# Top-k attention and a PReLU MLP in one kernel: when pairs are prepared and how the MLP's steps are paced

## The chip, the core and the metric

The kernel runs on one core of a Trainium2 chip. The metric is the device time of one execution in microseconds (us). The engines are PE (TensorE, matrix products), DVE (VectorE), ACT (ScalarE), POOL (GpSimd) and SP (SyncE, which here only issues DMAs). Each works off its own queue in order; they wait for each other through semaphores.

## The reference

```python
def _attn_ref(q, k, v):                     # 8 batches, 8 heads, 576 rows, head size 64
    scores = scale * np.matmul(q, k.transpose(0, 1, 3, 2))
    kth = np.partition(scores, -top_k, axis=-1)[..., -top_k:-top_k + 1]      # top_k = 32
    mask = scores >= kth
    scores = np.where(mask, scores, -1000000000.0)
    scores = scores - np.max(scores, axis=-1, keepdims=True)
    attn = np.exp(scores)
    attn = attn / (np.sum(attn, axis=-1, keepdims=True) + 1e-09)
    return np.matmul(attn, v)
def _moe_ref(x, w_in, w_out, alpha):        # x: 4608 tokens of 512; 2048 hidden
    h = x @ w_in
    g = np.maximum(h, 0.0) + alpha * np.minimum(h, 0.0)
    return g @ w_out
```

The attention's output, with its heads side by side, is the x of the MLP.

## The kernel before, in words

**Pairs, rows and ticks.** Two heads make a pair; there are 32 pairs, four to a batch. A pair has nine row blocks of 128 rows (four for each head, and a ninth made of the last 64 rows of both), so there are 288 row blocks. The program is written out by hand as a loop over ticks n (line 753). In tick n each engine gets its part for the row block that has reached it: PE the scores of block n+1 (line 314, two blocks at once, but the ninth of a pair alone), ACT the biased copy b (323), the sign count h (329) and the exponential e (334) of block n, POOL the sign SG, DVE the flip y of block n-1 (345), the segment maxima of block n-2 (355), the merge to the top values of block n-3 (370, 372), and the mask of block n-7 (419), which POOL multiplies with e (429). SP then transposes the weights by DMA, and three or four ticks later PE forms their product with v, av, into pu (488); DVE takes the reciprocal rz of the sums (505) and ACT writes the scaled result to xb (517). Within a tick PE's queue holds first the scores, then the step of the MLP, then everything that is listed for that tick under "pe": the preparation and the av products. On DVE the work listed under "dve" stands near the end of the tick, just ahead of the flip.

**Preparation.** `prep_plan(p)` lists 17 steps for a pair, each at a number of ticks before BASE[p], the due tick: transposes of q and k into qkT on PE with copies by ACT (lines 175 to 201, -14 to -11), a product of k with itself pg (206, -11) and its copy GK, the product pr of GK with q (218, -10), DVE's product P (226, -9), the statistics st (234, -7), and eight tiny DVE steps up to -2, which give NT, the estimate of each row's threshold that b needs. The loads of q and k are issued 18 ticks before BASE, those of v 13. BASE is 9p up to pair 27. Row blocks 252 to 287 belong to the last batch, whose four pairs are worked through side by side in an order of their own (ORDER, line 152); their due ticks are 247, 250, 254 and 258. qkT has 5 buffers, v 6, the staging tiles 2.

**The MLP.** `back` is a queue of steps. Each step has a PE part and an ACT part, `after`, which is run at the head of the next tick or just ahead of the next step. First come the steps that load and scale the weights; the last four, `w_id`, each add up 16 products into pl (596), and `w_id2` copies pl to w_id_b (600). Then come blocks of 512 or 128 tokens: `ph` steps (635), each four products of 512 columns, followed by ACT's gT (641), and after them, for each 128 tokens, three `pz` steps of up to seven products (649, 653), the last of them followed by ACT's copy o_sb (658) and the store. A 512-token block has 16 ph and 12 pz steps, a 128-token block 4 and 3. ph and pz share one PSUM bank, so that a step waits for the copy of the one before. Up to tick 251 every tick takes one step; from tick 252 a credit of 1.9 a tick (2.4 from tick 288) is spent at 0.9 for a ph and 1.5 for a pz.

**From attention to MLP.** When the last pair of a batch is finished, `x_turn` has SP transpose its xb by five DMAs into xT, the operand of ph (line 721, tick n+7), and `feed` appends the blocks that are complete to `back` (722, tick n+8), so that their first step stands one tick after that.

Of the kernel before, what the change touches and what calls it, by code (L numbers as in the profile page):

```python
# [16 lines left out]
S = 576  # L17
# [13 lines left out]
def kernel(  # L31
# [17 lines left out]
    NPAIR = (B * H) // 2  # L49
# [107 lines left out]
    while n < NT:  # L157
# [2 lines left out]
            unit_of[n + i] = (n, m, i)  # L160
        units.append((n, m))
        n += m
    BASE = {p: TPP * p for p in range(P0)}
    BASE.update({P0: N0 - 5, P0 + 1: N0 - 2, P0 + 2: N0 + 2, P0 + 3: N0 + 6})

    def prep_plan(p):
        d = pairs[p]
# [387 lines left out]
    def weight_steps():  # L555
        hold = {}

        def alpha():
            a16 = mlp.tile([NFT, 128], FP32, name="a16", bufs=1)
            nc.sync.dma_start(a16, moe_alpha.rearrange("(t p) -> t p", p=128))  # L560
            hold["a16"] = a16

        def alpha1():
            aps = ps_m.tile([128, NFT], FP32, name="aps", tag="misc")
            nc.tensor.transpose(aps, hold["a16"], ident_f[0:NFT, 0:NFT])
            hold["aps"] = aps
            hold["inT"] = mlp.tile([128, NKT, NFT, 128], BF16, name="w_inT", tag="gT", bufs=1)

        def alpha2():
            nc.scalar.copy(alpha_sb, hold["aps"])  # L570
            nc.gpsimd.tensor_scalar(alpha1m, alpha_sb, -1.0, 1.0, ALU.mult, ALU.add)

        def lin(f):
            return xT[:, f // 4, DM * (f % 4):DM * (f % 4 + 1)]

        def w_in(kk):
            for hf in range(0, DFF, 1024):
                nc.gpsimd.dma_start(w_in_b[:, kk, hf:hf + 1024],
                                    moe_w_in[kk * 128:(kk + 1) * 128, hf:hf + 1024])

        def w_in2(kk):
            nc.sync.dma_start_transpose(hold["inT"][:, kk, :, :], w_in_b[:, kk, :])

        def w_out(f):
            hold[f] = mlp.tile([128, DM], FP32, name="w_stage2", tag="stage", bufs=3)
            nc.sync.dma_start(hold[f], moe_w_out[f * 128:(f + 1) * 128, :])

        def w_out2(f):
            ws = hold.pop(f)
            nc.scalar.activation(w_out_b[:, f, :], ws, AF.Copy, scale=alpha1m[:, f:f + 1])  # L590
            nc.scalar.activation(lin(f), ws, AF.Copy, scale=alpha_sb[:, f:f + 1])

        def w_id(kk):
            hold["pl"] = pl = ps_m.tile([128, DM], FP32, name="pl", tag="misc")
            for f in range(NFT):
                nc.tensor.matmul(pl, hold["inT"][:, kk, f, :], lin(f),
                                 start=(f == 0), stop=(f == NFT - 1))

        def w_id2(kk):
            nc.scalar.copy(w_id_b[:, kk, :], hold["pl"])  # L600

        yield alpha, None
        yield (lambda: None), None
        yield (lambda: (alpha1(), w_out(0), w_out(1))), alpha2
        for f in range(NFT):
            yield ((lambda f=f: (w_out(f + 2) if f + 2 < NFT else None,
                                 w_in(f // 2) if f < 8 and f % 2 == 0 else None)),
                   (lambda f=f: w_out2(f)))
            yield (lambda: None), (lambda f=f: w_in2(f // 2) if f < 8 and f % 2 == 1 else None)
        for kk in range(NKT):  # L610
            yield (lambda kk=kk: w_id(kk)), (lambda kk=kk: w_id2(kk))

    banks = [0, 0]

# [8 lines left out]
    def mlp_steps(t0, tb):  # L623
        c0 = t0 % NX
        fpp = 512 // tb if tb <= 256 else 1
        hold = {}

        def ph_step(f):
            if f == 0:
                hold["gT"] = mlp.tile([128, NFT, 512], BF16, name="gT", tag="gT", bufs=1)  # L630
            ph = mlp_bank("ph", fpp * tb)
            hold[f] = ph.rearrange("p (f t) -> p f t", f=fpp)
            for i in range(fpp):
                for kk in range(NKT):
                    nc.tensor.matmul(hold[f][:, i, :],  # L635
                                     w_in_b[:, kk, (f + i) * 128:(f + i + 1) * 128],
                                     xT[:, kk, c0:c0 + tb],
                                     start=(kk == 0), stop=(kk == NKT - 1))

        def ph_act(f):  # L640
            nc.scalar.activation(hold["gT"][:, f:f + fpp, 0:tb], hold.pop(f), AF.Relu)  # L641

        def pz_step(r0, m, part):
            if part == 0:
                hold["pz"] = mlp_bank("pz", DM)
            pz = hold["pz"]
            for i in range(part * 7, min(part * 7 + 7, NKT + NFT)):
                if i < NKT:
                    nc.tensor.matmul(pz[0:m], xT[:, i, c0 + r0:c0 + r0 + m],  # L649
                                     w_id_b[:, i, :], start=(i == 0), stop=False)  # L650
                else:
                    f = i - NKT
                    nc.tensor.matmul(pz[0:m], hold["gT"][:, f, r0:r0 + m], w_out_b[:, f, :],  # L653
                                     start=False, stop=(f == NFT - 1))

        def pz_act(r0, m):
            o_sb = mlp.tile([128, DM], FP32, name="o_sb", tag="stage", bufs=3)
            nc.scalar.copy(o_sb[0:m], hold["pz"][0:m])  # L658
            if t0 == t7 - 64:
                nc.sync.dma_start(out[t0:t7, :], o_sb[0:64])  # L660
                nc.sync.dma_start(out[NTOK - 64:NTOK, :], o_sb[64:128])
            else:
                o0 = t0 + r0 - (64 if t0 > t7 else 0)
                nc.sync.dma_start(out[o0:o0 + m, :], o_sb[0:m])

        for f in range(0, NFT, fpp):
            yield (lambda f=f: ph_step(f)), (lambda f=f: ph_act(f)), 0.9
        for r0 in range(0, tb, 128):
            m = min(128, tb - r0)
            for part in range(3):  # L670
                yield ((lambda r0=r0, m=m, part=part: pz_step(r0, m, part)),
                       (lambda r0=r0, m=m: pz_act(r0, m)) if part == 2 else None, 1.5)

    blocks = []
    for i in range(0, 6 * S, 2 * S):
# [4 lines left out]
    last.update({i: (t7 + 64 + 128 * i, 128) for i in range(4)})  # L680
    assert sum(x[1] for x in blocks + list(last.values())) == NTOK

    PE_TICK = 1.9
    LAG_S, LAG_M, LAG_W = 2, 3, 7
    NW = NT - 6

# [1 line left out]
    with tc.manual_schedule(engines={E.PE, E.Activation, E.DVE, E.Pool, E.SP}):  # L688
        cal = {}

        def put(tick, eng, f):
            cal.setdefault((tick, eng), []).append(f)
# [15 lines left out]
        def tail_of(n, wn):  # L708
            wp, wj = ORDER[wn]
            b = wp // KPB  # L710
            if wp < P0:
                if wj == 3:
                    put(n + 3, "pe", lambda: av(wp, 0))
                    put(n + 4, "dve", lambda: av_rz(wp, 0))
                    put(n + 6, "act", lambda: av_out(wp, 0))
                if wj == 8:
                    put(n + 4, "pe", lambda: av(wp, 1))
                    put(n + 5, "dve", lambda: av_rz(wp, 1))
                    put(n + 7, "act", lambda: av_out(wp, 1))
                    if wp % KPB == KPB - 1:  # L720
                        put(n + 7, "end", lambda: x_turn(b, range(5)))
                        put(n + 8, "end", lambda: feed((b + 1) * S))
            elif (wj == 8 or wj % 2) and wp % 2:
                i, g = (wj // 2, (wp - P0) // 2)
                dt = 4 if n < NT else 2
                put(n + dt, "pe", lambda: av_last(i, g))
                put(n + dt + 1, "dve", lambda: rz_last(i, g))
                put(n + dt + 1, "dvx", lambda: out_last(i, g))
                if g == 1:
                    put(n + dt + 1, "dvx", lambda: x_turn(b, (i,)))  # L730
                    put(n + dt + 3, "end",
                        lambda: back.extend(mlp_steps(*last.pop(i))))
# [9 lines left out]
            for eng in ("act", "pool", "pe", "dve"):  # L742
                run(t, eng)
        scores(0)
        back = deque((a, c, 1.0) for a, c in weight_steps())
        credit = 0.0
        after = None
        wdue, held = {}, []
# [3 lines left out]
        end = max(NT + 24, 0)  # L752
        while n < end or back or after:
            for p in range(2, NPAIR):
                if n == max(0, BASE[p] - (18 if p < P0 else 17)):
                    load(p)
                    plan(p)
                if n == max(0, BASE[p] - 13):
                    load_v(p)
# [20 lines left out]
            run(n, "act")  # L780
            if n >= 3 and n % 3 == 0 and n - 3 < NT:
                sel_a((n - 3) // 3)
            credit = min(credit, 0.0) + (2.4 if n >= NT else PE_TICK if n >= N0 else 0.0)
            first = n < N0
            while back and (first or credit > 0.0):
                first = False
                if after:
                    after()
                pe_f, after, cost = back.popleft()
                pe_f()  # L790
                credit -= cost if n >= N0 else 0.0
            run(n, "pe")
            due = wdue.get(n, ())
            for wn in due:
# [179 lines left out]
```

## Time and profile before

| | |
|---|---|
| median of three runs | 927.65 us (926.9 to 927.79) |
| profiled execution | 929.21 us, span 927.4 us |
| mean granted clock of TensorE | 0.908 |
| DMA | 99.52 MB, 107 GB/s on average |
| idle time of POOL ahead of w (429) | 375.3 us in 250 |
| idle time of ACT ahead of gT (641) | 41.8 us in 144, all for ph |
| idle time of ACT ahead of o_sb (658) | 39.4 us in 36, all for pz |

The span is the time from the first instruction to the last on the device; about 1.8 us of an execution lies around it. Busy times are shares of the span. A wait is given as the engine and line that stood still, the engine and line whose result came last, then the total in us, the number of times and the longest. In a timeline, the bracket behind a row is the idle time of its engine just ahead of it and what ended it.

### The profile page before, as it was taken

The numbers are of one execution on the slowest core, as the hardware profiler recorded it, in microseconds if no ns is written. First come the engines' busy times: TensorE is split into PE (matmuls) and PEld (weight loads), VectorE is DVE, ScalarE is ACT, GpSimd is POOL, SyncE is SP. The second block draws the span as 40 slices with busy tenths as digits, with TensorE's granted clock in tenths as the row PEclk, the third lists the DMA queues.
The fourth block names the chain that finished last, engine by engine and source line by source line (L and its number), as shares of the span: only waits on it lengthen the run. The fifth ranks groups of instructions, "written<-read, shape, count | busy, mean of one in ns | idle before, by whom it ended". The sixth has DMA issues, their size and how long they took to land.

```text
span 927.4 us, 20789 instructions
## 1 busy us (share of the span) xinstructions
PE 752.0 (81%) x5702; PEld 448.4 (48%) x5779; DVE 847.7 (91%) x5305; ACT 810.4 (87%) x1873; POOL 431.0 (46%) x629
## 2 busy tenths in 40 slices
PE   5866797678977788878986889787986788989996
PEld 3544444344543445544553455544553444544564
DVE  3899969999999999999999999999999888999970
ACT  4999979799897999999897998999997988879842
POOL 0364534544554455555555454555554434455510
PEclk9565788799997999999977999999987999979999
DMA  6699634544556555564546546464456843353551
GB/s 149 121 174 200 132 65 86 105 93 91 124 106 111 92 103 110 115 115 93 126 99 124 95 88 126 97 125 94 106 126 103 146 85 74 76 101 62 115 94 45
DMA packets 343021, 99.52 MB, mean 107 GB/s; under 512 B 335200, under 2 KB 335216, under 8 KB 342896
## 3 DMA queue, kind: packets, MB, share of 16 engines
q1 hardware_dynamic: 340544, 95.71, 52.5%
q0 software_dynamic: 1152, 2.10, 1.6%
q8 instruction: 48, 0.79, 0.4%
q14 instruction: 77, 0.63, 0.2%
q10 hardware_dynamic: 1200, 0.30, 0.2%
HBM read 36.71 MB, written 9.44 MB: 50 GB/s over the span
## 4 chain that ended last, share of the span: by engine, by line
ACT 42%; PE 26%; DVE 24%; issue 3%; DMA 2%; POOL 1%; SPq 1%; ACTq 0%
ACT b L323 10%; ACT h L329 9%; ACT e L334 8%; DVE C L355 7%; PE ps L314 7%; PE pz L653 7%; PE ph L635 5%; ACT gT L641 4%; DVE mk L419 4%; DVE y L345 4%; DVE C L372 3%; DVE L L370 3%; ACT xb L517 2%; PE pz L649 2%; PE pg L206 2%
## 5 line engine op out<-in xcount | busy, mean ns | idle before, releaser
L429 POOL TENSOR_TENSOR w<-mk,e 128x576 bf16<-128x576 bf16 x250 | 319.2, 1277 | 375.3 <-DVE mk L419 208.3
L355 DVE MAX8 C<-y 128x8 f32<-128x96 f32 x1728 | 421.1, 244 | 0.1
L314 PE MATMUL ps<-qkT 64*128 64x288 f32 (+1 forms) x1280 | 255.9, 478 | 26.3 <-ACT b L323 26.1
L323 ACT ACTIVATE b<-ps,NT 128x576 f32<-128x576 f32 x288 | 201.5, 755 | 3.2 <-PE ps L314 3.2
L329 ACT ACTIVATE h<-b 128x576 bf16<-128x576 f32 x288 | 202.0, 701 | 2.0
L635 PE MATMUL ph<-xT,w_in_b 128*128 128x128 bf16 (+1 forms) x920 | 151.5, 302 | 54.4 <-ACT gT L641 27.2
L314 PEld LDWEIGHTS ps<-qkT 64*128 64x128 f32 (+1 forms) x1280 | 135.4, 195 | 86.4 <-ACT b L323 46.7
L334 ACT ACTIVATE e<-b 128x1152 bf16<-128x1152 f32 (+1 forms) x158 | 173.8, 1100 | 0.0
L370 DVE MAX8 L<-C 128x8 f32<-128x48 f32 x864 | 163.8, 190 | 0.1
L345 DVE TENSOR_SCALAR y<-b,SG 128x576 int32<-128x576 int32 x288 | 147.5, 512 | 10.0 <-POOL SG L339 9.4
L419 DVE TENSOR_SCALAR mk<-b,KP 128x576 bf16<-128x576 f32 x282 | 143.8, 510 | 0.0
L653 PE MATMUL pz<-w_out_b,gT 128*128 128x512 bf16 x551 | 134.2, 379 | 4.1 <-issue 3.0
L635 PEld LDWEIGHTS <-w_in_b 128*128 128x128 bf16 x960 | 70.8, 99 | 124.0 <-issue 93.9
L641 ACT ACTIVATE gT<-ph 128x512 bf16<-128x512 f32 x144 | 87.8, 618 | 41.8 <-PE ph L635 41.7
L372 DVE MATCH_REPLACE8 C<-L,C 128x48 f32<-128x48 f32 x576 | 109.1, 189 | 0.0
L653 PEld LDWEIGHTS <-gT 128*128 128x128 bf16 x576 | 52.7, 98 | 68.6 <-issue 13.1
L488 PE MATMUL pu<-v_bf,wT 128*128 128x65 bf16 (+1 forms) x1600 | 71.0, 201 | 11.0 <-DMA wT<-w 8.4
L339 POOL TENSOR_SCALAR SG<-S_all 128x1 int32<-128x1 f32 x288 | 65.2, 227 | 27.8 <-ACT h L329 27.5
L488 PEld LDWEIGHTS <-wT 128*128 128x128 bf16 (+1 forms) x1600 | 66.2, 105 | 24.6 <-DMA wT<-w 8.9
L429 POOL TENSOR_TENSOR wm<-mk,e 128x576 bf16<-128x576 bf16 x32 | 40.8, 1276 | 49.7 <-DVE mk L419 47.9
L329 ACT ACTIVATION_READ_ACCUMULATOR h<-b 128x1 f32 x288 | 61.6, 214 | 0.0
L658 ACT COPY o_sb<-pz 128x512 f32<-128x512 f32 x36 | 21.3, 591 | 39.4 <-PE pz L653 39.4
(102 smaller groups left out, 838.0 us busy)
## 6 DMA issues: line engine op xcount, KB each, us to landing
out_dram<-o_sb SPq DMA_DIRECT2D x35, 256.0 KB, 2.2
st_q<-in_q_dram SPq DMA_DIRECT2D x64, 128.0 KB, 2.9
st_v<-in_v_dram SPq DMA_DIRECT2D x64, 128.0 KB, 2.6
kst<-in_k_dram SPq DMA_DIRECT2D x62, 128.0 KB, 2.8
w_stage<-in_moe_w_out_dram SPq DMA_DIRECT2D x16, 256.0 KB, 3.1
w_in_b<-in_moe_w_in_dram POOLq DMA_DIRECT2D x8, 256.0 KB, 6.8
wT<-w SPq DMA_TRANSPOSE x128, 3.3
st_q<-in_q_dram SPq DMA_DIRECT2D x32, 32.0 KB, 2.8
```

The costliest lines, as they stand in the source:

```text
L314: nc.tensor.matmul(o_, l_, r_, start=True, stop=True)
L323: nc.scalar.activation(t["b"].rearrange("p (a c) -> p a c", a=2), t["ps"], AF.Identity, bias=NT0[:, p * TPP + j:p * TPP + j + 1], scale=ON ...
L329: nc.scalar.activation(h, tiles[n]["b"], AF.Sign, accum_out=S_all[:, n:n + 1])
L334: nc.scalar.activation(e, tiles[n0]["bu"], AF.Exp, scale=scl)
L345: nc.vector.tensor_scalar(t["y"].bitcast(I32), t["b"].bitcast(I32), FLIP, SG[:, n:n + 1], ALU.bitwise_xor, ALU.bitwise_xor)
L355: return [lambda g=g: nc.vector.max(out=C[:, n % TPP, g, :], in_=t["y"][:, g * SEG:(g + 1) * SEG]) for g in range(NSEG)]
L370: ops.append(lambda r=r, src=src: nc.vector.max(out=L[:, 8 * r:8 * r + 8], in_=src))
L419: nc.vector.tensor_scalar(t["mk"], t["b"], row_limit(n), None, ALU.is_ge)
L429: nc.gpsimd.tensor_tensor(dst, t["mk"], t["e"], ALU.mult)
L488: nc.tensor.matmul(o_, wT[:, 4 * side + c, cs], d["v"][:, 5 * side + c, :], start=(c == 0), stop=(c == 4))
L635: nc.tensor.matmul(hold[f][:, i, :], w_in_b[:, kk, (f + i) * 128:(f + i + 1) * 128], xT[:, kk, c0:c0 + tb], start=(kk == 0), stop=(kk == N ...
L653: nc.tensor.matmul(pz[0:m], hold["gT"][:, f, r0:r0 + m], w_out_b[:, f, :], start=False, stop=(f == NFT - 1))
```

## The change

There are four edits.

1. BASE becomes one formula, min(9p, 258 - 8(31 - p)): up to pair 10 nothing changes, from there a pair is due every eight ticks. Pair 27 moves from tick 243 to 226, pair 28 from 247 to 234, pair 29 from 250 to 242, pair 30 from 254 to 250; pair 31 stays at 258. The loads of all pairs are issued 18 ticks ahead (17 before for the last four).
2. After each `w_id` step stands an empty step, and the copy `w_id2` belongs to the empty one: it is run one tick later, and the four products stand two ticks apart.
3. `feed` is called at tick n+9.
4. A step has two costs, one for the ticks up to 251 and one for those from 252. The first are 1.0 for weight steps, 1.0 for ph and 0.7 for pz, against a credit of 1.0 a tick; a pz then shares a tick with another in three ticks out of seven. The second are as before.

```diff
-    BASE = {p: TPP * p for p in range(P0)}
-    BASE.update({P0: N0 - 5, P0 + 1: N0 - 2, P0 + 2: N0 + 2, P0 + 3: N0 + 6})
+    BASE = {p: min(TPP * p, N0 + 6 - 8 * (P0 + 3 - p)) for p in range(NPAIR)}
...
-            yield (lambda kk=kk: w_id(kk)), (lambda kk=kk: w_id2(kk))
+            yield (lambda kk=kk: w_id(kk)), None
+            yield (lambda: None), (lambda kk=kk: w_id2(kk))
...
-            yield (lambda f=f: ph_step(f)), (lambda f=f: ph_act(f)), 0.9
+            yield (lambda f=f: ph_step(f)), (lambda f=f: ph_act(f)), (1.0, 0.9)
...
-                       (lambda r0=r0, m=m: pz_act(r0, m)) if part == 2 else None, 1.5)
+                       (lambda r0=r0, m=m: pz_act(r0, m)) if part == 2 else None, (0.7, 1.5))
...
-    PE_TICK = 1.9
+    LOAD_AT = 18
...
-                        put(n + 8, "end", lambda: feed((b + 1) * S))
+                        put(n + 9, "end", lambda: feed((b + 1) * S))
...
-        back = deque((a, c, 1.0) for a, c in weight_steps())
+        back = deque((a, c, (1.0, 1.0)) for a, c in weight_steps())
...
-                if n == max(0, BASE[p] - (18 if p < P0 else 17)):
+                if n == max(0, BASE[p] - LOAD_AT):
...
-            credit = min(credit, 0.0) + (2.4 if n >= NT else PE_TICK if n >= N0 else 0.0)
-            first = n < N0
-            while back and (first or credit > 0.0):
-                first = False
+            late = n >= N0
+            credit = min(credit, 0.0) + (2.4 if n >= NT else 1.9 if late else 1.0)
+            while back and credit > 0.0:
                 if after:
                     after()
                 pe_f, after, cost = back.popleft()
                 pe_f()
-                credit -= cost if n >= N0 else 0.0
+                credit -= cost[late]
```

By the code, the MLP blocks of the first seven batches then start one tick later, and a 512-token block takes 24 or 25 ticks instead of 28. The last step of the whole queue stands at tick 301 in both.

## The prediction, made before the result was known

> **What bounds the kernel now.** I read the page's shares first, then the busy time in 40 slices.
>
> ```profile
> PE 752.0 (81%) x5702; PEld 448.4 (48%) x5779; DVE 847.7 (91%) x5305; ACT 810.4 (87%) x1873; POOL 431.0 (46%) x629
> ...
> DVE  3899969999999999999999999999999888999970
> ACT  4999979799897999999897998999997988879842
> ```
>
> VectorE (DVE) is full except at the ends, in slice 6, and from slice 32 to 35. So the question for every edit is whether it removes or makes DVE idle time. A table by stage gives it: span, then busy time of each engine. All windows but the fourth and the last run from one y (the flip, one a tick) to the y nine ticks later.
>
> ```profile
> core 0: us, PE busy (x) PEld busy (x) DVE busy (x) ACT busy (x) POOL busy (x), PEclk, DMA share, GB/s
> 101.00:131.20 30.20, 22.55 (x128) 13.45 (x127) 26.14 (x164) 25.86 (x60) 13.54 (x20) 0.77 0.50 96
> 131.20:163.30 32.10, 26.00 (x213) 15.67 (x215) 26.90 (x172) 27.52 (x63) 13.47 (x19) 0.89 0.37 75
> 189.90:216.80 26.90, 20.67 (x160) 11.90 (x163) 25.91 (x164) 26.12 (x64) 13.47 (x19) 1.00 0.45 90
> 647.00:680.00 33.00, 31.33 (x237) 17.95 (x241) 32.71 (x209) 30.52 (x74) 17.75 (x25) 1.00 0.55 119
> 719.50:753.10 33.60, 27.11 (x216) 16.15 (x217) 27.75 (x172) 30.37 (x75) 13.57 (x19) 0.95 0.71 133
> 753.10:785.40 32.30, 26.20 (x201) 14.33 (x203) 27.91 (x177) 26.60 (x64) 13.51 (x19) 1.00 0.31 59
> 785.40:813.30 27.90, 26.19 (x249) 15.41 (x249) 25.97 (x167) 22.69 (x52) 13.50 (x19) 1.00 0.41 83
> 889.20:927.40 38.20, 31.07 (x350) 21.34 (x351) 11.08 (x50) 10.70 (x18) 0.00 (x0) 0.95 0.32 69
> ```
>
> An ordinary stretch (third row) takes 26.9 us for nine ticks, 2.99 a tick, and DVE idles 26.9 - 25.91 = 0.99. Four stretches are worse: idle 4.06 and 5.20 at ticks 27 to 45, where the weights' linear product w_id runs, and 5.85 and 4.39 at ticks 234 to 252, where five pairs are prepared. The first nine ticks of the last four pairs (785.4) idle 1.93. After 889.2 only the end of the MLP is left, 38.2 us in which PE is busy 31.07. The waits say for whom DVE stood still; the rows are from the windows 101 to 163 (three), 719 to 813 (three) and 45 to 719 (the last).
>
> ```profile
> DVE P L226 <- PE pr L218: 4.1, 1, 4.1
> DVE rz L505 <- PE pu L488: 3.8, 1, 3.8
> DVE sq L251 <- ACT MM L247: 1.3, 1, 1.3
> ...
> DVE rz L505 <- PE pu L488: 6.5, 5, 2.3
> DVE y L345 <- POOL SG L339: 2.6, 3, 1.6
> DVE P L226 <- PE pr L218: 2.5, 4, 1.0
> ...
> DVE P L226 <- PE pr L218: 11.4, 14, 4.1
> ```
>
> Nearly all of it is PE being late with something that DVE wants one tick later. PE's queue is in order and the MLP step of a tick stands ahead of the preparation and the AV product of that tick. So I ask of each edit: how late is PE, and how much lateness is covered.
>
> **1. Linear matrix copied a tick later.** The timeline at the four products (PE, ACT and DVE):
>
> ```profile
> 124.08 3.40 PE L596 MATMUL pl<-xT,w_inT 128*128 128x512 bf16 x15 [0.16 <-issue]
> 127.86 0.82 DVE L226 TENSOR_TENSOR P<-pr,qTb 128x512 bf16<-128x512 f32 x2 [4.06 <-PE pr L218]
> 128.16 3.61 PE L596 MATMUL pl<-xT,w_inT 128*128 128x512 bf16 x16 [0.31 <-ACT w_id_b L600]
> 131.81 0.59 ACT L600 CAST w_id_b<-pl 128x512 bf16<-128x512 f32 x1 [1.58 <-PE pl L596]
> 132.87 3.63 PE L596 MATMUL pl<-xT,w_inT 128*128 128x512 bf16 x15
> ```
>
> One product is 3.6 us of PE in a 2.95 us tick, four ticks in a row, and ACT stops for each before it may make the next b. With an empty step between, a product has 5.9 us, in which PE also has one pair of score rows (1.24), and ACT's copy comes a tick after the product was queued. Nothing is added but four empty steps; the queue is empty by tick 43 and the first MLP block comes later than that. The first stall stays: the product at tick 35 still stands ahead of pr, for which DVE waits 4.06. The second and third (3.8 and 1.3) go: 5.1. Bounds: 0 (the stall only moves) to 5.2, all the idle time of that window. I take 5.1.
>
> **2. Pairs prepared every eight ticks.** Before, pairs 27 to 31 are prepared at due ticks 243, 247, 250, 254, 258; after, at 226, 234, 242, 250, 258. From pair 11 on each is due earlier than before except pair 31, so no work is added and pair 31 is due as before. Between ticks 234 and 261 DVE idles 5.85 + 4.39 + 1.93 = 12.2 us. If these 27 ticks become ordinary ones, 3 x 0.99 = 3.0 stays: 9.2 gained. Bounds: 4 (the rz waits, 6.5 us, are AV's and go only in part) to 12.2. I take 9.2. The buffers allow it: qkT of pair p-5 is read last four ticks or more before pair p takes it (pair 31: tick 241 against 245), v of p-6 six ticks before. The loads (six DMAs a pair, and four for v) move with their pair on SP's queue, still four and five ticks ahead of their first reader.
>
> The price is paid from tick 84 to 229: a pair every eight ticks instead of nine, while ACT is busy 26.12 of 26.9. The larger of its copies for a pair:
>
> ```profile
> L183 ACT CAST v_bf<-st_v 128x640 bf16<-128x640 f32 x32 | 23.3, 730 | 0.0
> L192 ACT COPY qkT<-pk 128x512 f32<-128x512 f32 x32 | 19.5, 608 | 1.2 <-PE pk L188 1.2
> L178 ACT COPY qkT<-pq 128x512 f32<-128x512 f32 x32 | 18.7, 584 | 6.9 <-PE pq L175 6.9
> ```
>
> with the second copy of pq as long as the first, these are 2.5 us; an eighth instead of a ninth of it is 0.035 us a tick, 0.3 in nine, against 0.78 idle. It fits, but a pair's copies now meet the AV copies at another row each time. I take 1.0, from -1 (pr leaves the single row, its worst place) to +4.
>
> **3. Feed one tick later.** The block's first ph is queued before its transposes are in. The start of one MLP, PE, ACT and DVE:
>
> ```profile
> 701.53 1.37 ACT L323 ACTIVATE b<-ps,NT 128x576 f32<-128x576 f32 x2
> 706.04 0.59 PE L635 MATMUL ph<-xT,w_in_b 128*128 128x512 bf16 x1 [4.75 <-DMA xT<-xb]
> 707.94 0.60 ACT L641 ACTIVATE gT<-ph 128x512 bf16<-128x512 f32 x1 [3.71 <-PE ph L635]
> 709.85 0.52 DVE L345 TENSOR_SCALAR y<-b,SG 128x576 int32<-128x576 int32 x1
> 712.61 0.74 ACT L323 ACTIVATE b<-ps,NT 128x576 f32<-128x576 f32 x1
> 716.79 0.51 DVE L345 TENSOR_SCALAR y<-b,SG 128x576 int32<-128x576 int32 x1
> ```
>
> ACT runs ahead: the b of 701.53 is flipped at 709.85, 8.3 us later. Then PE waits 4.75 for the transposes, ACT 3.71 for PE, and the b of 712.61 is flipped 4.2 us later, with no lead left. Queued a tick later, the ph still starts when the transposes land, but behind the next scores, and ACT makes the next b before it waits; I work out some 4 us of lead kept. The lead does not shorten anything itself; it covers PE's lateness. Of the P waits above, 11.4 - 4.1 = 7.3 us fall in the MLP stretches. I count 5.5 of them covered (bounds 0 and 7.3). In the last stretch the ph steps wait for the same landing, so the end moves with DVE.
>
> **4. MLP paced by step length.** This is the edit that costs. Up to tick 251 one step a tick becomes a credit of 1.0, a ph costing 1.0 and a third of a pz 0.7: ten pz parts in seven ticks, most often two in one tick. A pz part on PE:
>
> ```profile
> 649.75 1.24 PE L314 MATMUL ps<-qkT 64*128 64x288 f32 x8
> 650.92 1.68 PE L653 MATMUL pz<-w_out_b,gT 128*128 128x512 bf16 x7
> 652.44 0.60 PE L188 MATMUL pk<-ident_f,kst 128*128 128x128 f32 x4
> ```
>
> It takes 652.44 - 650.92 = 1.52 us. In the fourth row of the table (11 flips, pz throughout, one part a tick) PE is busy 31.33 of 33.0, 2.85 a tick, so 1.33 without pz. Ten parts in seven ticks are 2.17, together 3.50 against a tick of 2.99: PE falls behind by 0.5 us a tick, over the 12 parts of a 512-token block (8.4 ticks) 4.2 us. There are five whole such stretches before tick 252 and most of a sixth. If nothing covers it, that is 6 x 4.2 = 25 us; if the kept lead covers it, 0. Blocks that follow a long pause (those of the first, second, fourth and sixth batch) start with the 4 us of lead; I charge them 0.5 each. Two blocks (1152, 2304) come six ticks after the last; they start with little lead, and I charge 3.5 each, 7. With 2 in all for those: 9.
>
> *Sum*: -5.1 - 9.2 + 1.0 - 5.5 + 9.0 = -9.8. The profiled execution took 929.2 us (span 927.4), so 919.4; it lay 1.6 above the median of the three runs, 927.65, so **918 us**.
>
> A rule that speaks against edit 4 stands in the Trainium skill, "TensorE: Matmul & The Clock Gate", Part 1: the array's clock is halved after about 3.4 us of little activity and comes back after as long a busy time. The trace agrees where the MLP starts anew:
>
> ```profile
> 706.00:712.00 6.00, 5.74 (x18) 2.28 (x20) 6.00 (x41) 3.41 (x10) 3.74 (x6) 0.52 0.55 122
> 712.00:720.00 8.00, 6.68 (x46) 4.30 (x45) 7.34 (x43) 7.10 (x16) 3.32 (x6) 1.00 1.03 136
> ```
>
> **The rivals.**
> *A, slower*: the lead isn't kept, and PE's lateness in the pz stretches goes to DVE whole. Then edit 3 gives 0 and edit 4 costs 25: 929.2 - 5.1 - 9.2 + 1 + 25 = 940.9, 939 in the median's terms. It decides from the point where a pz stretch costs over (5.1 + 9.2 - 1)/6 = 2.2 us without lead. For it: the w_id stretch, where overload of PE did turn into DVE idle time, 9.2 us. Against it: DVE idles 0.29 in the 33 us of pz with PE at 95%, so some cover is there already.
> *B, faster*: the lead covers everything: -5.1 - 9.2 + 1 - 7.3 = -20.6, 907 us. For it: 8 us of lead in MLP-free ticks. Against it: blocks 1152 and 2304.
> *C, no change*: the eight-tick spacing does not do what it says, because the rz waits come from AV behind the MLP step and not from the crowd; only 4 of 9.2 is gained, and the denser preparation costs 4: 929.2 - 5.1 - 4 + 4 - 5.5 + 9 = 927.6, 926.
> *D, the clock*: a finished MLP leaves longer pauses, six ticks before blocks 1152 and 2304 where there was one, so PE starts both at a clock of 0.52. A window of 6 us at 0.52 does 3 us less work; put wholly on DVE, twice 3: 924. This is what the gate of that page would make here.
>
> **How the numbers follow.** About 0.2% (1.9 us, so 925.8 and 929.5) is what a measurement can tell from no change. Forecast 0.45 (own range 912 to 925), A 0.21, B 0.18, C 0.08, D 0.08. Faster: forecast, B, D, together 0.71; same: C, 0.08; slower: A, 0.21. Low end 906 (B, with a little from the first bound of part 2), high end 932, at which A is half weighed: a stretch costing 3 us instead of 4.2 and a little lead.
>
> **What would show it.** Ticks 131 to 163 shrink to about 27 us, with no ACT wait for pl, and one P wait of some 4 us stays. Ticks 234 to 252 take 54 to 56 instead of 66. The PE wait for xT shortens, and gT no longer waits 3.7 us at the start of an MLP. In the pz stretches PE is over 97% busy and DVE waits for pu, pr or SG; if DVE idles over 2.2 us in each, A is right; under 0.5, B. The stretch after the last flip stays at 38 us; if it grows by 2 or more, the later feed reached the end, which I excluded.

## The result, and the profile after

The changed kernel takes 973.69 us (median of 4), the one before 927.72: a ratio of 1.048, with a 95% interval of 1.044 to 1.052. The prediction was 918, and not even its slow rival, 939, comes near. The profiled execution has a span of 971.6 us, 44.2 more than before.

The page of the changed kernel, the same three rows:

```profile
PE 789.7 (81%) x5779; PEld 462.1 (48%) x5779; DVE 851.3 (88%) x5305; ACT 814.3 (84%) x1873; POOL 431.2 (44%) x629
...
DVE  3899989999999888988799988898889989999980
ACT  4999989998889888987797888797879888889842
```

DVE has the work that it had, 851 us against 848, and is idle where it was full: in the middle, where the digits are 8 and 7. Its stages, from one y to the y nine ticks later except the last row, stand for ticks 27, 36, 54, 72, 99, 135, 234, 243 and 252 and what follows the last y:

```profile
101.20:131.70 30.50, 23.14 (x120) 14.26 (x118) 25.85 (x163) 28.57 (x66) 13.48 (x19) 0.72 0.46 94
131.70:158.50 26.80, 23.37 (x211) 14.09 (x211) 26.70 (x172) 24.39 (x58) 13.50 (x19) 0.99 0.45 90
184.30:210.10 25.80, 20.45 (x161) 11.60 (x160) 25.80 (x163) 25.02 (x62) 13.48 (x19) 1.00 0.51 95
236.20:265.30 29.10, 24.32 (x202) 15.12 (x200) 26.88 (x171) 24.22 (x57) 13.51 (x19) 0.82 0.51 106
318.10:350.50 32.40, 28.73 (x196) 16.00 (x192) 26.46 (x164) 25.98 (x63) 13.52 (x19) 0.95 0.46 96
440.60:474.90 34.30, 30.90 (x210) 16.65 (x210) 27.11 (x165) 27.34 (x64) 13.55 (x19) 0.90 0.49 94
769.90:799.70 29.80, 23.82 (x174) 12.76 (x173) 26.26 (x164) 26.03 (x62) 13.53 (x19) 0.89 0.50 96
799.70:830.50 30.80, 27.46 (x198) 14.69 (x196) 26.40 (x164) 26.54 (x64) 13.53 (x19) 1.00 0.39 65
830.50:856.70 26.20, 25.77 (x250) 15.09 (x246) 25.95 (x167) 24.17 (x56) 13.47 (x19) 1.00 0.44 89
932.60:971.60 39.00, 32.16 (x367) 22.29 (x364) 11.11 (x50) 11.30 (x19) 0.00 (x0) 0.99 0.32 74
```

The second row is the w_id stretch: 26.8 instead of 32.1, as predicted. The third is the first ph stretch after the later feed: DVE never idle, 25.8 instead of 26.9. Ticks 234 to 252 take 60.6 instead of 65.9, a gain, though a smaller one. But the stretches at ticks 99 and 135 take 32.4 and 34.3, with DVE idle for 5.9 and 7.2. In the kernel before, the same nine ticks took 26.3, with DVE idle for 0.4:

```profile
323.40:349.70 26.30, 23.54 (x178) 13.24 (x181) 25.91 (x164) 25.19 (x62) 13.48 (x19) 1.00 0.55 108
428.20:454.50 26.30, 23.54 (x178) 13.24 (x180) 25.91 (x164) 25.19 (x62) 13.49 (x19) 1.00 0.50 107
```

In stretches like these, from tick 90 on, the time went. The waits of DVE in the changed kernel from 265 to 800 us:

```profile
DVE y L344 <- POOL SG L338: 19.6, 12, 3.1
DVE rz L504 <- PE pu L487: 15.4, 18, 1.8
DVE P L225 <- PE pr L217: 11.6, 15, 2.3
DVE sq L250 <- ACT MM L246: 9.1, 10, 1.7
```

They sum to 56 us, on four different results, all of which PE makes or ACT copies from PE; that PE is the one that is late is so far a reading. One such place in the changed kernel, PE, then ACT and DVE:

```profile
452.59 1.26 PE L487 MATMUL pu<-v_bf,wT 128*128 128x65 bf16 x20 [1.09 <-ACT xm L516]
453.78 2.29 PE L313 MATMUL ps<-qkT 64*128 64x288 f32 x8
456.00 1.89 PE L649 MATMUL pz<-w_id_b,xT 128*128 128x512 bf16 x4
457.68 2.75 PE L653 MATMUL pz<-w_out_b,gT 128*128 128x512 bf16 x10
460.26 0.60 PE L174 MATMUL pq<-ident_f,st_q 128*128 128x128 f32 x4
...
460.90 0.59 ACT L177 COPY qkT<-pq 128x512 f32<-128x512 f32 x1 [3.43 <-PE pq L174]
...
462.99 0.52 DVE L344 TENSOR_SCALAR y<-b,SG 128x576 int32<-128x576 int32 x1 [3.09 <-POOL SG L338]
```

PE first waits 1.09 for the copies that free a bank of pu, then runs two pz parts in one tick, 4.3 us from 456.00 to 460.26, and only then the transposes pq. ACT's copy of pq stands ahead of the sign count that gives SG, so ACT stops for 3.43, and DVE's flip for 3.09. A prepared pair and a double pz step had not met like this before the change. The rows hold a second cause: the eight score products take 2.29 and the first four pz products 1.68, where the rows in part 4 of the prediction have 1.24 for eight and 1.52 for seven. Part of the lateness is thus a slower PE; the last section comes back to it.

### The profile page after: what moved, and what is told of

Its sections match the earlier page's. It is cut to its first block, busy times and chain, and to the rows that moved or that the text cites. A ratio compares the mean times of both kernels' runs of the same rounds, so it can differ in the third digit from the quotient of the medians.

```text
span 971.6 us, 20853 instructions
## 1 busy us (share of the span) xinstructions
PE 789.7 (81%) x5779; PEld 462.1 (48%) x5779; DVE 851.3 (88%) x5305; ACT 814.3 (84%) x1873; POOL 431.2 (44%) x629
## 3 DMA queue, kind: packets, MB, share of 16 engines
q0 software_dynamic: 1152, 2.10, 1.6%
## 4 chain that ended last, share of the span: by engine, by line
PE 35%; ACT 30%; DVE 30%; issue 2%; DMA 2%; POOL 1%; SPq 0%; ACTq 0%; POOLq 0%
PE pz L653 10%; DVE C L354 9%; ACT b L322 8%; PE ps L313 8%; ACT h L328 5%; ACT e L333 5%; PE ph L635 5%; DVE y L344 4%; DVE mk L418 4%; DVE C L371 3%; ACT gT L641 3%; DVE L L369 3%; PE pz L649 3%; PE pu L487 3%; PE pg L205 2%
## 5 line engine op out<-in xcount | busy, mean ns | idle before, releaser
L313 PE MATMUL ps<-qkT 64*128 64x288 f32 (+1 forms) x1280 | 265.0, 496 | 28.5 <-ACT b L322 28.1
L635 PE MATMUL ph<-xT,w_in_b 128*128 128x128 bf16 (+1 forms) x960 | 161.1, 313 | 37.5 <-ACT gT L641 31.5
L313 PEld LDWEIGHTS ps<-qkT 64*128 64x128 f32 (+1 forms) x1280 | 138.8, 204 | 95.6 <-ACT b L322 48.6
L653 PE MATMUL pz<-w_out_b,gT 128*128 128x512 bf16 x576 | 138.1, 383 | 0.0
L653 PEld LDWEIGHTS <-gT 128*128 128x128 bf16 x576 | 54.7, 99 | 70.8 <-issue 11.9
L487 PE MATMUL pu<-v_bf,wT 128*128 128x65 bf16 (+1 forms) x1600 | 72.8, 203 | 14.1 <-DMA wT<-w 6.5
L487 PEld LDWEIGHTS <-wT 128*128 128x128 bf16 (+1 forms) x1600 | 67.5, 106 | 26.3 <-issue 12.9
L205 PE MATMUL pg<-kst 128*128 128x130 f32 x320 | 55.5, 333 | 11.5 <-ACT qTb L200 11.1
```

The costliest lines, as they stand in the source:

```text
L313: nc.tensor.matmul(o_, l_, r_, start=True, stop=True)
L487: nc.tensor.matmul(o_, wT[:, 4 * side + c, cs], d["v"][:, 5 * side + c, :], start=(c == 0), stop=(c == 4))
L635: nc.tensor.matmul(hold[f][:, i, :], w_in_b[:, kk, (f + i) * 128:(f + i + 1) * 128], xT[:, kk, c0:c0 + tb], start=(kk == 0), stop=(kk == N ...
```

## The experiments

The runs are given with their medians; the kernel before lay at 928.0 to 929.1 in the same sets.

### Which edit costs

Four runs set the new due ticks or the new pacing into the kernel before, or take one of them out of the changed one.

```diff
+# only_base: the kernel before with (and all loads 18 ticks ahead)
+    BASE = {p: min(TPP * p, N0 + 6 - 8 * (P0 + 3 - p)) for p in range(NPAIR)}
+# only_pace: the kernel before with the costs (1.0, 0.9), (0.7, 1.5), and a credit of 1.0
+# wid_feed: the kernel before with the empty step after w_id, and feed at n + 9
+# pace_one: the changed kernel with
-                       (lambda r0=r0, m=m: pz_act(r0, m)) if part == 2 else None, (0.7, 1.5))
+                       (lambda r0=r0, m=m: pz_act(r0, m)) if part == 2 else None, (1.0, 1.5))
```

> The kernel before with the new BASE formula and its load ticks alone. Theory S (the spacing is what costs: a pair's copies fall on another row each time and meet the AV copies on ACT): 945 us or more, with DVE waits for SG of over 10 us between 265 and 800. Theory P (two pz parts in a tick cost it all, the spacing is good): about 918 us, as part 2 of the prediction has it. Theory X (only the two together cost): 918 to 930.

> The kernel before with the two costs per step and the credit of 1.0 alone. Theory P: 950 us or more, DVE idle 4 us in each of six pz stretches. Theory S: 925 to 935. Theory X: 930 to 945, rival A's 25 us without lead being its upper end.

> The kernel before with the linear matrix copied a tick later and the feed a tick later, spacing and pacing as before. All theories: parts 1 and 3 of the prediction, -5.1 and -5.5, about 917 us. If the feed's lead is worth nothing, 922; if the later feed costs at the end, 925.

> The changed kernel with the early cost of a pz put at 1.0, so that one step is taken a tick; spacing, linear matrix and feed stay changed. Theory S: 950 us or more. Theory P: 910 to 920. Theory X: 915 to 930.

The spacing alone: 958.16, ratio 1.033 (1.028 to 1.038). The pacing alone: 963.13, 1.038 (1.032 to 1.045). Linear matrix and feed: 915.52, 0.987 (0.981 to 0.993). The changed kernel with one step a tick: 942.08, 1.016 (1.010 to 1.021). So neither theory that puts it all on one edit holds, nor the one that needs both together: by themselves the spacing costs 30 and the pacing 35, and the two other edits are worth 12.5, where the prediction gave them 10.6. The sign that theory S named did not come: in only_base, DVE waits 7.0 us for SG between 265 and 800, not over 10, and more for pu (14.1) and pr (11.6).

The same set of edits with the old due ticks, and the feed by itself:

```diff
+# old_base: the changed kernel with (and the loads as before)
+    BASE = {p: TPP * p for p in range(P0)}
+    BASE.update({P0: N0 - 5, P0 + 1: N0 - 2, P0 + 2: N0 + 2, P0 + 3: N0 + 6})
+# only_feed: the kernel before with
+                        put(n + 9, "end", lambda: feed((b + 1) * S))
```

> The changed kernel with the old due ticks: linear matrix, feed and pacing as changed. If the lead of the later feed covers PE's lateness in pz stretches (part 4 of the prediction): 915.5 of the run without pacing plus 9, 925. If nothing is covered: plus the 35 us that pacing alone cost, 950. I expect 930 to 940, half of it covered, since the first pz stretch of the changed kernel lost 2.3 us and that of pacing alone some 4.5.

> The kernel before with the feed one tick later alone. Part 3 of the prediction: the waits for pr in the MLP stretches go, 5.5 to 7.5 us, 920.5 to 922.5. If the two edits of the run that has both only work together, 925 to 928.

old_base took 939.71 and only_feed 920.2 (ratio 0.9915, 0.9892 to 0.9938). wid_feed was run again for its interval:

> The same kernel as the run with linear matrix and feed as changed, spacing and pacing as before, for an interval: 913 to 918, ratio about 0.987.

914.78, ratio 0.985 (0.983 to 0.987). With these the sum of the change can be written in runs: feed 928.1 to 920.2, -7.9; linear matrix 920.2 to 914.8, -5.4; pacing 914.8 to 939.7, +24.9; spacing 914.8 to 942.1, +27.3; the two together 7 more than their sum, to 973.7. Most of these are medians of two runs that lie 0.6 to 3.7 us apart, so a single step is good to some 3 us, and the 7 is little more than that.

### Why the spacing costs: density or place

```diff
+# shift_six: the kernel before with
-    BASE = {p: TPP * p for p in range(P0)}
+    BASE = {p: TPP * p - (6 if p > 10 else 0) for p in range(P0)}
```

> The kernel before, with pairs 11 to 27 due six ticks earlier but still nine ticks apart. Theory M (meeting: what costs is where a pair's preparation falls against the AV work; a pair six ticks early has its copy of v in the same tick as the AV product and two sets of AV copies, the place of the largest waits, 2.0 for SG and 0.5 for pu): 1.5 to 2.5 us in each of some 13 pairs that meet an MLP stretch, 945 to 958 us. Theory D (density: a pair every eight ticks is too much work for PE and ACT, wherever it falls): no denser than before, 925 to 931.

975.65, as much as the whole change. Apart from pairs 10 and 11, which are three ticks apart, nothing is denser here, so density does not explain this cost: it is the place. (Whether density adds to the cost of the spacing of eight is not settled by this run.) But which meeting was it? Two runs took the suspected ones away.

```diff
+# six_v_later: shift_six, with act_v of pairs 11 to 27 at
-                                                             -3, -2, -8]
+                                                             -3, -2, -7 if 10 < p < 28 else -8]
+# six_av_later: shift_six, with the second AV product and its followers a tick later
+                    put(n + 5, "pe", lambda: av(wp, 1))
+                    put(n + 6, "dve", lambda: av_rz(wp, 1))
+                    put(n + 8, "act", lambda: av_out(wp, 1))
+                        put(n + 8, "end", lambda: x_turn(b, range(5)))
+                        put(n + 9, "end", lambda: feed((b + 1) * S))
```

> The run with pairs 11 to 27 six ticks early (975.7 us), and of these pairs the copy of v, alone, one tick later, out of the tick with the AV product and its two sets of copies. Theory M: the waits of DVE for SG (19.8 us in 18 between 265 and 800) mostly go, those for pu in the second tick of a pair (av1 behind pg) stay: 955 to 965. If ACT is simply full, the tick does not matter: 973 to 978.

> The run with pairs 11 to 27 six ticks early, and the AV product of a pair's last five row blocks one tick later (with its reciprocal, copies, transposes and feed), out of the tick of pg and away from the copy of v. Theory M: both the waits for pu in the second tick and those for SG shrink by half or more: 940 to 958. If PE is simply full, the wait moves one tick and stays: 970 to 978.

974.13 and 999.0: both misses. In the first the wait for SG fell from 19.8 to 11.3 us, and that for pu rose from 22.0 to 28.4; a cause further up was only handed to another wait. In the second it became worse. So neither of the two suspected meetings is the cause. What I had not looked at is whom PE itself waits for. In shift_six, from 265 to 800:

```profile
PE pr L218 <- DVE P L226: 44.2, 18, 4.1
```

In the two runs that missed, it was still there: in six_v_later it stands at 43.0 in 18, and in six_av_later it has passed from pr to pu,

```profile
PE pu L488 <- DVE P L226: 27.8, 15, 3.2
```

One of the 18 places in shift_six, PE, ACT and DVE:

```profile
424.85 1.24 PE L488 MATMUL pu<-v_bf,wT 128*128 128x65 bf16 x30
426.03 1.04 PE L635 MATMUL ph<-xT,w_in_b 128*128 128x512 bf16 x4
426.99 0.41 PE L218 MATMUL pr<-qTb,GK 64*64 64x512 bf16 x2
430.00 0.22 PE L218 MATMUL pr<-qTb,GK 64*64 64x64 bf16 x2 [2.60 <-DVE P L226]
430.14 1.24 PE L314 MATMUL ps<-qkT 64*128 64x288 f32 x8
...
429.27 0.68 DVE L226 TENSOR_TENSOR P<-pr,qTb 128x512 bf16<-128x512 f32 x1
...
435.55 0.52 ACT L517 ACTIVATE xm<-pu,rz 64x64 bf16<-64x64 f32 x2
```

pr consists of two tiles, 512 and 64 columns wide. They come from the pool ps_d, tag pd, of two buffers, and so do st and pu. A rule of the Trainium skill says why there are two tiles: in "PSUM — Partial Sum Buffer", section "PSUM: the matmul accumulator", one product may fill at most one bank, 512 fp32 columns, and here are 576; no run here tries a wider one. pu takes one buffer at 424.85 and keeps it until its last copy ends at 436.07, 11.2 us. The first pr takes the other. The second has none, and waits until DVE has read the first; DVE does that in the next tick, because P is listed there. Everything behind it on PE, the scores among it, stands still for 2.6 us. In the kernel before, pr falls between the copies of one pu and the product of the next:

```profile
630.66 1.00 ACT L517 ACTIVATE xb<-pu,rz 128x64 bf16<-128x64 f32 x4
...
636.01 0.43 PE L218 MATMUL pr<-qTb,GK 64*64 64x512 bf16 x4
...
640.23 1.24 PE L488 MATMUL pu<-v_bf,wT 128*128 128x65 bf16 x30
```

By the code, a pu is alive at seven of the nine places of a pair. pr needs two places in a row, its own and the next, in which DVE reads it, and the due tick of 9p puts it at the first of the two that are left: the only place at which it meets no pu.

### The test: other banks, everything else as it was

```diff
+# six_pa, every_6_pa, eight_pa
-                pr = ps_d.tile([128, n1 - n0], FP32, name="pr", tag="pd")
+                pr = (ps_a.tile([128, n1 - n0], FP32, name="pr", tag="pa") if n0 else
+                      ps_d.tile([128, n1 - n0], FP32, name="pr", tag="pd"))
+# six_pa2, eight_pa2, after_pa2: that, and
-            st = ps_d.tile([128, 2, TPP], FP32, name="st", tag="pd")
+            st = ps_a.tile([128, 2, TPP], FP32, name="st", tag="pa")
```

The bank of the transposes (tag pa) is free from pg's copy on until the next pair's first transpose.

> The run with pairs 11 to 27 six ticks early (975.7 us), with the second, 64-column tile of pr in the PSUM bank of the transposes (tag pa) in place of the pool that it shares with st and pu. Theory B (banks: pu holds one of the pool's two banks from the AV product to its copies three ticks later; pr, which takes both, must wait for DVE's P in the next tick, with everything on PE behind it): PE's wait ahead of pr for P goes, 45 us to under 3, and the time falls to 935 to 955. Theory M (meeting of work on ACT and PE): 970 or more.

> As the run before it, with st moved to that bank too. Theory B: st can't stand in the way of pu either, 928 to 945. Theory M: 970 or more.

> Linear matrix and feed as changed, pairs every eight ticks, one step a tick, and pr's second tile and st in the bank of the transposes (pace_one, with the banks moved, 942.1 us). Theory B: what the spacing costs mostly goes, and the gain at ticks 234 to 261 is kept: 905 to 918. Theory M: 938 or more.

> The changed kernel with pr's second tile and st in the bank of the transposes. Theory B: what is left over is the pacing, 905 to 918 plus 24 of the run with the old due ticks, 929 to 942. Theory M: 968 or more.

six_pa: 931.69, 44 of the 48 us that shift_six had lost, and faster than expected of the theory of banks; six_pa2 935.68. PE's wait ahead of pr for P is gone from six_pa's waits between 265 and 800. In six_pa (one line longer, so its line numbers are one higher) pr runs through with a pu alive:

```profile
409.08 1.24 PE L489 MATMUL pu<-v_bf,wT 128*128 128x65 bf16 x30
410.25 1.04 PE L636 MATMUL ph<-xT,w_in_b 128*128 128x512 bf16 x4
411.22 0.43 PE L219 MATMUL pr<-qTb,GK 64*64 64x512 bf16 x4
411.58 1.24 PE L315 MATMUL ps<-qkT 64*128 64x288 f32 x8
```

eight_pa2: 928.49 against the 942.08 of pace_one; after_pa2: 952.29 against 973.69. So the banks are 14 us of the 27 that the spacing of eight costs, and 21 us in the changed kernel. The changed kernel's trace had the same kind of wait, PE ahead of pr, from 265 to 800:

```profile
PE pr L217 <- DVE P L225: 13.0, 7, 3.9
PE pr L217 <- ACT xm L516: 6.6, 4, 2.6
```

With pu's own waits for a reader of the pool (6.6 in 7) that makes 26.2; in after_pa2 6.5 of it is left, all of pu, and the transposes wait 4.2 for st in their bank.

The rest was not settled. Both runs with the spacing of eight miss what the theory of banks expected of them, 905 to 918 and 929 to 942. six_pa loses next to nothing with its pairs nine ticks apart, so for what is left of the cost of eight the theory of density is still open. Its largest piece is ticks 90 to 99, 29.6 us in eight_pa2 as in pace_one and 25.8 in wid_feed. A small part is the moved bank itself: the first nine ticks take 30.1 in place of 28.5. st left in its old pool changes nothing:

> As eight_pa2 (928.5 us), but st stays in its old pool. six_pa was 4 us faster than six_pa2, since st in the bank of the transposes makes the next pair's first transpose wait for its copy: 920 to 927. If st in the old pool stands in the way of pu at the moving places: 929 to 936.

928.95. With the banks moved the pacing costs 24 us (952.29 - 928.49), as it does with the old due ticks; with the old banks and the spacing of eight it cost 32 (973.69 - 942.08). So with the banks moved nothing is left of the 7 us by which the two together exceeded their sum.

### A version that beats both

```diff
+# every_6: wid_feed with (and all loads 18 ticks ahead)
+    BASE = {p: min(TPP * p, N0 + 6 - 6 * (P0 + 3 - p)) for p in range(NPAIR)}
+# every_7: the same with 7 in place of 6; every_6_pa: every_6 with the edit of six_pa
```

> Linear matrix and feed as changed, one step a tick, and pairs 25 to 31 due six ticks apart, so that only the last seven move. Theory M: few pairs leave their place, and they fall where no MLP runs or at the old crowd: 915.5 less 3 to 7, 909 to 913. If any move of a pair costs 1.5 to 2.5 us as in the spacing of eight: 5 pairs, 915 to 922.

> As the run with six, but pairs 21 to 31 seven ticks apart. Theory M: the crowd is thinner still, but pairs 21 to 25 leave their place while an MLP runs: 912 to 920. Theory D: 910 to 914, between six and nothing.

> Linear matrix and feed as changed, one step a tick, pairs 25 to 31 six ticks apart, and pr's second tile in the bank of the transposes. Theory B: the 10.3 us that PE waited for P in the run with six (915.7 us) go, and with them the 4 us of DVE idle time around ticks 216 to 225 and part of that at 234: 906 to 912, the fastest. If the banks matter only for pairs in the midst of an MLP: 914 to 917.

With six: 915.68, no gain over wid_feed. With seven: 930.69, which no theory had expected. Its trace loses from tick 171 on, where the first of the moved pairs is prepared: ticks 171 to 234 take 204.5 us in place of the 182.9 of wid_feed, and ticks 234 to 261 win 8.6 back. No run with seven has the banks moved, so how much of that is the banks is open. With six and the bank: 911.38, ratio 0.981 (0.979 to 0.984), the fastest, if only by 3.4 us and with an interval that touches that of wid_feed. Its ticks 234 to 261:

```profile
711.60:739.20 27.60, 22.74 (x179) 13.17 (x177) 27.31 (x173) 26.82 (x68) 13.48 (x19) 1.00 0.51 102
739.20:766.20 27.00, 23.66 (x187) 12.85 (x186) 26.11 (x166) 24.45 (x60) 13.51 (x19) 1.00 0.39 77
766.20:793.20 27.00, 25.98 (x228) 14.87 (x227) 25.94 (x167) 22.83 (x51) 13.45 (x19) 1.00 0.49 86
```

81.6 us instead of the 93.8 of before: the gain that part 2 of the prediction had looked for. But it is not what the kernel gains. wid_feed takes 93.1 for these ticks, so 11.4 are won; the 27 ticks before them, into which pairs have moved, take 82.8 in place of 78.8, and the first nine 30.2 in place of 28.5. Some 6 us are left in the two profiles, 3.4 in the medians.

## Why the prediction was wrong

The forecast was 918 and 973.7 came, 56 us more. Two terms of its sum failed, both of them prices: the 1.0 for the spacing and the 9.0 for the pacing. The gains that stood beside them came, near to what was forecast.

*Part 1, linear matrix.* Right: 5.1 forecast, 5.4 measured; one P wait of 3.8 to 4.7 us stayed.

*Part 3, feed.* Right in mechanism, a little low: 5.5 forecast with a bound of 7.3, 7.9 measured. In only_feed, as in the third row of the stages above, DVE is never idle in the ph stretches. The end hardly moved: 39.0 us after the last flip against 38.2.

*Part 4, pacing.* Wrong was the cover. I charged 9 with the lead; the runs show 25. The overload of PE itself was worked out nearly right. Stage by stage, in us, with the block whose MLP falls into the ticks (wid_feed by its second profile; the charge is in the prediction's text):

| ticks | block | charged | before | only_pace | wid_feed | old_base |
|---|---|---|---|---|---|---|
| 54 to 81 | 0 | 0.5 | 80.0 | 84.7 | 78.6 | 81.0 |
| 81 to 117 | 512 | 0.5 | 106.5 | 113.2 | 104.2 | 109.0 |
| 117 to 153 | 1152 | 3.5 | 104.9 | 111.4 | 104.2 | 110.0 |
| 153 to 189 | 1664 | 0.5 | 106.4 | 111.8 | 104.1 | 108.6 |
| 189 to 225 | 2304 | 3.5 | 105.2 | 110.8 | 104.6 | 110.0 |
| 225 to 261 | 2816 | 0.5 | 120.4 | 122.4 | 118.9 | 120.5 |

Without the later feed the pacing costs 30.9 in these ticks, where I had 25. (The medians have 35; in the profile of only_pace, ticks 18 to 27, ahead of any block, take 31.5 in place of 27.0, with PE waiting 6.2 for a DMA, so that much of it need not be pacing.) With the later feed it costs 24.5. The four blocks that I charged 0.5 each lost 2.4, 4.8, 4.5 and 1.6, the two that I charged 3.5 lost 5.8 and 5.4. So the lead took off about 6, not 16 of 25.

Why it covers so little is not shown. That P and rz are taken straight from PE, while the lead is ACT's, would be a reason, but the waits do not bear it out. From only_pace to old_base, between 236 and 800 us, DVE's waits for P, straight from PE, fell from 28.9 to 12.7, those for rz rose from 7.9 to 11.0, and those for SG, through ACT, from 1.6 to 7.3. A clock that fell in the pz stretch is not the reason either, at least in the first block: old_base has a granted clock of 1.00 from 211.3 to 251.6, and its waits of that block end at 240.96 and 251.04. Rival A's 25 is met, but its reason, a lead that isn't kept, is not. Rival D's 3 us at the start of blocks 1152 and 2304 did not come either: at the first, ticks 117 to 135 take 52.9 in place of 51.6, with a clock of 1.00 from tick 126 to 135.

*Part 2, spacing.* The gain at ticks 234 to 252 was there: pace_one takes 55.5 us for them, inside the 54 to 56 that I named, and 83.1 for ticks 234 to 261, where wid_feed takes 93.1. The price was not 1 but some 37, since the 27 are net of that gain. "The buffers allow it" is the step that failed: I checked the SBUF buffers, qkT and v, and did not check PSUM, and it was true only for the pools I had counted. I even took leaving the place of 9p for a possible gain ("pr leaves the single row, its worst place"); it was the only place at which pr meets no pu. Of the price, 14 us are shown to be the banks, 21 in the changed kernel; what the rest is stays open. I also bounded the price by ACT's busy time, an average, though what moved was above all at which of nine places the work falls. The profile of before had next to no row for it (1.7 us of PE ahead of pr for P), since the tuned place hardly met the limit; the code had it, in one tag shared by three tiles.

*Small readings.* DVE is below full in slices 32 to 34, not to 35. Two pz parts share a tick in three ticks of seven, not most often. Of the sixth stretch, half the parts stand before tick 252 and not most of them; it lost the least.

## What to carry over

Before a step is moved in a hand-written schedule, list what it allocates, PSUM above all, who else draws on the same pool, and from when to when each holds it. When a wait disappears from one engine and comes back on another, as here from SG to pu, the cause lies further up: ask whom the late engine itself was waiting for. And slack that one engine has built up is not a credit against which another engine's overload can be set off: here it took off 6 us of 31.

## What was not expected of the hardware

In the place of the changed kernel shown first, the four products of 512 columns from 456.00 to 457.68 took 0.42 us each; in the kernel before, the seven whose row the prediction shows took 1.52 in all, 0.22 each. The granted clock around it:

```profile
444.90:448.30 3.40, 3.40 (x31) 1.80 (x28) 2.79 (x18) 2.60 (x8) 1.34 (x2) 1.00 0.00 0
448.30:451.70 3.40, 1.64 (x18) 0.87 (x16) 3.40 (x21) 3.40 (x9) 1.60 (x3) 1.00 0.49 92
451.70:458.50 6.80, 5.91 (x34) 3.16 (x34) 6.80 (x44) 5.14 (x14) 3.43 (x6) 0.50 0.40 81
458.50:475.00 16.50, 16.50 (x97) 8.73 (x95) 10.78 (x69) 12.29 (x30) 5.72 (x8) 1.00 0.65 123
```

PE ran at half its clock from 451.70 to 458.50, in the midst of an MLP. In the 3.4 us ahead of that it had been busy for 1.64, so it need not stand still for long for this to happen. The wait for the bank, from 451.50 to 452.59, had hardly begun when the clock fell, so it cannot have been the cause by itself; ahead of it PE had waited 1.55 for gT. The scores and the four products took 1.05 and 0.8 us longer than at the full clock, so of the 3.09 that DVE waited there some 1.9 can be the clock, by this estimate. Between 265 and 800 us the mean granted clock is 0.89, where it was 0.94 before the change; what the half clock adds to the 44 us was not measured by itself.
